# A linear-attention and token-mixing kernel on one core: another hand-written order, the products of v off GpSimd

## The chip, the cores and the metric

The kernel runs on one core of a Trainium2 chip. The metric is device time in microseconds (us) of one execution. TensorE is called PE in the profile (its weight loads PEld), VectorE DVE, ScalarE ACT, GpSimd POOL, and SyncE SP; SP issues all loads and stores here.

## The reference

Eight batches of eight heads; a sequence of 576 tokens, 64 numbers a head. First a linear attention with cosine weights, then a layer that mixes tokens:

```python
theta = np.pi / 2.0 * pos / S
def phi(x, c, s):
    r = np.maximum(x, 0.0)
    return np.concatenate([r * c, r * s], axis=-1)
q_p = phi(q, cos_w, sin_w); k_p = phi(k, cos_w, sin_w)
kv = np.einsum('bhsf,bhsd->bhfd', k_p, v)
z = np.sum(k_p, axis=2)
num = np.einsum('bhsf,bhfd->bhsd', q_p, kv)
den = np.einsum('bhsf,bhf->bhs', q_p, z)[..., None] + 1e-06
...
wq = x @ w_q; wk = x @ w_k
W_tok = scale * np.einsum('bsd,btd->bst', wq, wk)
mixed = np.einsum('bst,btd->bsd', W_tok, x)
return (np.maximum(mixed, 0.0) @ w_out)
```

Here `x` is num / den with the heads side by side, 8 x 576 x 512.

## The kernel before, in words

The work is cut into 16 groups H of four heads (two groups a batch). The order of all work is written out by hand: `ORDER` is a list of words such as `VS9a` or `KV11:6` or `RK9@A`. The letters name a step, the number its group, `a` or `b` one half of it, the number behind the colon the bank of PSUM that it starts in, and the letter behind `@` the engine (A ScalarE, V VectorE, G GpSimd). The kernel issues the steps in that order, and each engine works through its own in order; the framework adds the waits that the data and the buffers ask for.

One group passes through these steps:

- `LQ`, `LK`, `LV`: two loads of 288 KB each, issued by SP into one of four raw buffers.
- `RQ`, `RK` (lines 198 and 200): relu of q and k with conversion to bf16, on any of three engines, whole or by halves.
- The weighted v. The weights are put on v in place of k: `vtab` holds sine and cosine. Either `CV` converts v to bf16 (lines 204, 206, 208) and `VS` multiplies it on VectorE (line 229), or `VG` multiplies the raw v on GpSimd (line 243). The result is in one of two buffers `v2`.
- `KV` (line 280, or 270 in wide tiles): TensorE sums k'v over the tokens; `KE` moves the result to SBUF.
- `QT` (line 296, or 290 in wide tiles): TensorE transposes q; `QM` (line 315, wide 311) multiplies it by its weights on VectorE.
- `N` (line 335): numerator and denominator of half a group, g = 2H + r; `EP` (346 on ScalarE, 348 on VectorE) adds eps to the denominator, `RC` (line 367) or, for both halves at once, `RJ` (line 370) takes the reciprocal, `X` (line 382) multiplies: 32 such products of x.
- `XT` or `XR` (lines 395, 408) transposes x, `XE` copies it to SBUF.

A batch b then has `WK`, `KW`, `WQ`, `QW` (the two projections and their copies), `KX`, `XK`, `XA`, `XB` (the product of wk and x, and its copies across the halves of the partitions), four times `MX` and `ME` (mixing and its relu, line 478 and 489 or 491). Two batches make nine output tiles: `WO` (line 498, four products each), `OE` (the copy from PSUM) and `ST` (the store). `WU` (line 534) multiplies a constant tile of ones; nothing uses the result. `TK`, `TV`, `TQ`, `TW`, `T2`, `TZ`, `TI`, `TB` prepare tables and constants.

A step on one engine thus waits for its data and for its buffer to be free: `VS` and `VG` of group H wait until `KV` of group H - 2 has read its `v2`.

Of the kernel before, what the change touches and what calls it, by code (L numbers as in the profile page):

```python
# [29 lines left out]
RK2b@A WK0:4 VG5a RJ3 X6 RK2a@A QT2:0 KW0@A X7 LQ5a LQ5b LK5b LK5a LV4b LQ4b LV7b LV4a KV2:6 QM2  # L30
XT3:2 VG5b KE2@A RQ5@A XE3@V N4:0 N5:6 EP4@V RC4 WQ0:2 EP5@A X4 RK5b@A KX0:3 VG4b RK5a@A RC5 QT5:0
X5 XK0@A KV5:4 QW0@A QM5 XA0@A LK4b LQ4a LQ7a LK4a LQ7b LV7a XT2:2 XB0@A KE5@A CV7b@A MX1:6 VG4a
XE2@V N11:0 RQ4b@A N10:4 EP11@V ME1@A WK1:2 EP10@V RJ5 RQ4a@A X10 MX0:6 WQ1:3 KW1@A X11 RK4b@A
RQ7a@G QT4:4 KX1:2 ME0@A RK4a@G QM4 QW1@A RQ7b@G LK7b LK7a LQ6a LW3 LV6a LW2 KV4:6 XK1@A XA1@A VS7b
QT7:2 KE4@A MX3:4 VG7a N9:6 QM7 ME3@A N8:0 XB1@A WU13:4 EP9@A RK7@A MX4:4 EP8@V RJ4 XT5:2 X9 ME4@A
X8 KV7:6 CW3@A VG6a XE5@V MX6:4 KE7@A LW4 LQ6b LW5 LV6b LK6b LV9b LK6a XR4:0 ME6@A MX2:6 XE4@V N15:2
CW2@A N14:4 ME2@V RQ6a@A WK2:0 EP14@A EP15@V RQ6b@A MX5:6 CW4@G RJ7 WQ2:1 KW2@V ME5@A CW5@G X15
KX2:0 QW2@A VG6b X14 MX7:6 XK2@A QT6:2 ME7@A WO0:1 QM6 XB2@A RK6b@A LQ9b LQ9a LV9a LK8b LV8b LV8a
WO3:0 RK6a@A LK8a LK9b OE0:0@V XA2@G VG9b MX10:2 OE3:1@A MX8:6 KV6:4 ME8@V ME10@A XR7:0 KE6@V RQ9b@A
MX9:6 MX11:2 XE7@V WO8:4 ME9@A RQ9a@V ME11@A CV9a@G N12:6 LK9a LQ8a LQ8b LQ11a OE8:2@A N13:0 VS9a  # L40
QT9:2 LV11a WO2:4 VG8b QM9 CV8a@A WO10:5 EP12@A EP13@A LQ11b LK10a OE2:3@A RJ6 WO1:2 X13 OE10:4@A
RK8@G X12 WO6:3 RK9@A VS8a XR6:6 KV9:0 LV11b LQ10a LQ10b OE1:5@V RQ8b@G KV8:4 LV10a OE6:6@V KE9@A
RQ8a@G N18:0 XE6@V KE8@A LK11a N19:2 VG11a QT8:4 EP19@V EP18@V WK3:6 RJ9 RQ11b@A QM8 WO12:7 KW3@A
WO7:6 X19 LK11b LV10b LK10b OE12:7@A VG11b RK10a@A KX3:7 LV13b LV13a OE7:8@V RQ11a@A WQ3:2 X18 XK3@A
N17:4 XB3@A QW3@V N16:6 EP17@A VG10a LV12b ST1 XR9:0 RQ10@A EP16@V RJ8 WO9:2 XE9@V RK11@A WO11:3 X16
X17 QT11:0 VG10b LV12a LK13a LK12a OE11:9@A WO4:6 LK13b OE9:10@A QM11 XR8:2 LK12b OE4:11@A QT10:0
MX15:4 RK10b@A XE8@V KV11:6 CV13@G ME15@A QM10 ST6 WK4:2 XA3@A KE11@A CV12b@G KV10:4 KW4@A VS13
MX14:2 KE10@A MX13:0 N23:6 ME14@A KX4:4 ME13@A VS12b MX12:2 XK4@A WQ4:5 VG12a EP23@V ME12@A RC23 X23
N21:0 QW4@A N20:2 RK13@A EP21@V WO15:5 EP20@V RJ10 X20 LQ12b LQ13a LQ13b LQ12a ST3 ST11 WO16:4 ST12
OE15:5@A RK12b@G X21 XA4@A RK12a@G N22:2 XB4@A MX16:6 LV14b LQ14a OE16:6@A XR10:0 EP22@V RC22  # L50
RQ13a@G ME16@A X22 KV12:4 RQ13b@G KV13:6 XE10@V KE12@A RQ12b@A MX17:4 RQ12a@G LV15b LQ14b ST10
QT13:2 KE13@V ME17@A XR11:0 QM13 QT12:6 XE11@A WO13:4 QM12 WO14:5 LV15a LQ15a ST9 OE13:7@A CV14b@G
MX19:0 N26:2 LQ15b OE14:9@V N27:6 WK5:4 EP26@V EP27@V RJ13 VG15b X26 WO5:5 KW5@A ME19@A X27 ST0
LK15b LK15a KX5:4 OE5:1@A WQ5:0 XK5@V VS14b MX18:6 QW5@A XR13:4 ME18@A N24:2 VG15a N25:0 XE13@A
WO19:6 EP25@V RC25 X25 WO21:7 EP24@A XA5@A RC24 LV14a ST14 LK14a LK14b OE19:0@A X24 WO20:0 RQ14@G
OE21:10@A RQ15a@V XR12:6 ST21 OE20:4@A RQ15b@G MX20:2 QT14:4 XE12@V ME20@A RK15@G ST15 WO17:0 QM14
WK6:1 VG14a ST4 ST8 ST2 OE17:9@A QT15:6 KW6@A KV15:4 QM15 RK14a@A WQ6:1 XB5@A KE15@A KX6:0 QW6@A
RK14b@G MX22:6 XK6@A N31:4 ME22@V MX23:2 EP31@A ST16 ST17 ST7 ST5 KV14:0 ME23@A RC31 X31 MX21:6
KE14@A N30:2 ME21@A N28:0 EP30@V N29:4 RC30 EP28@A X30 WO22:6 EP29@A RJ14 WO23:7 X29 OE22:6@A XB6@A
X28 WO24:6 XA6@A OE23:8@A XR15:0 MX25:4 XR14:2 XE15@V ME25@A WO18:7 XE14@V WO26:0 ST23 ST22 OE24:1@V  # L60
WK7:1 OE18:9@V OE26:3@A MX26:2 KW7@V MX27:4 MX24:6 ME27@A WQ7:0 ME26@V KX7:1 ME24@A QW7@A WO25:2
XK7@A XB7@A XA7@G WO29:3 ST18 ST19 ST26 OE25:9@V MX28:0 MX29:6 MX30:4 ME28@V WO30:2 ME30@A ME29@V
ST25 ST24 ST20 OE29:3@A MX31:4 WO27:0 OE30:0@V ME31@A WO32:1 ST30 OE27:9@A WO34:0 ST29 ST27 OE32:1@V
# [6 lines left out]
def kernel(  # L70
# [256 lines left out]
    def N(g, ps, eng):  # L327
        H, r = divmod(g, 2)
        place["N", g] = ps
        nv = num4(ps)[:, r::2] if H in NUM_JOINT else num(ps)  # L330
        for u in range(SC):
            for s in range(2):
                for pr in range(2):
                    a = slice(H2 * pr, H2 * pr + H2)
                    nc.tensor.matmul(  # L335
                        nv[:, pr, u, :], qm_b[H % NQM][a, s, r, 2 * u:2 * u + 2, :],
                        kv_b[H % 2][a, r, pr if H in KV_WIDE else 0, s, 0:D + 1],
                        start=(u == 0 and s == 0), stop=(u == SC - 1 and s == 1))
# [4 lines left out]
    def EP(g, ps, eng):
# [3 lines left out]
        else:  # L347
            V.tensor_scalar(rec(g), den, EPS, None, op0=ALU.add)

    def EJ(H, ps, eng):  # L350
# [4 lines left out]
        else:  # L355
            V.tensor_scalar(dst, den, EPS, None, op0=ALU.add)

# [6 lines left out]
            op=ALU.mult)  # L364

    def RC(g, ps, eng):
        V.reciprocal(rec(g), rec(g))

    def RJ(H, ps, eng):
        V.reciprocal(rec_b[H % 4], rec_b[H % 4])  # L370
# [91 lines left out]

# [122 lines left out]
```

## Time and profile before

| | |
|---|---|
| runs | 124.07, 126.06, 126.73 us; median 126.06 |
| the profiled execution | 122.76 us, its span 120.9 us |
| busy in the span | PE 95.1, PEld 64.4, DVE 95.4, ACT 81.0, POOL 68.3 us |
| moved by DMA | 39.40 MB, mean 326 GB/s; 29.62 MB read, 9.44 MB written |
| granted clock of TensorE | 0.984 |

The span runs from the first to the last instruction of that one execution; the 1.9 us between it and the time of 122.76 lie around it. The busy shares are means over a start (loads come in), a middle and an end (output tiles). So the prediction reads them stage by stage.

### The profile page before, as it was taken

How to read it: one execution, taken by the hardware profiler on the slowest of the kernel's cores; microseconds unless marked ns; L12 is line 12 of the kernel's file. 1: busy time of each engine (PE TensorE's matmuls, PEld its weight loads, DVE VectorE, ACT ScalarE, POOL GpSimd, SP SyncE). 2: the span in 40 equal slices, each digit the busy share in tenths (PEclk: the TensorE clock that was granted, in tenths of full speed). 3: DMA queues.
4: the chain of work that ended last, by engine and by line, in shares of the span. 5: the costliest groups of instructions: out<-in, count | busy, mean ns of one | idle time of the engine just before them, and what ended most of it. 6: DMA issues, size and time to landing. Idle time of an engine off the chain costs nothing.

```text
span 120.9 us, 5257 instructions
## 1 busy us (share of the span) xinstructions
PE 95.1 (79%) x2243; PEld 64.4 (53%) x2256; DVE 95.4 (79%) x143; ACT 81.0 (67%) x157; POOL 68.3 (57%) x65
## 2 busy tenths in 40 slices
PE   0005779799794999959996999678999999999950
PEld 0004568587573686543954586254765875554410
DVE  0089887999799989999896999987979887946440
ACT  6307925769992989967479589766488886367210
POOL 7500079399997796995699919959994000010000
PEclk9999999999998599999999999999999999999999
DMA  3999999999999999999999999997352990466992
GB/s 99 371 389 404 396 361 355 394 390 390 395 392 378 370 367 386 397 391 389 387 393 399 398 396 338 378 400 280 110 180 89 342 350 14 174 266 260 373 386 111
DMA packets 20663, 39.40 MB, mean 326 GB/s; under 512 B 3232, under 2 KB 3232, under 8 KB 20640
## 3 DMA queue, kind: packets, MB, share of 16 engines
q1 hardware_dynamic: 20640, 39.07, 87.4%
q8 instruction: 17, 0.28, 0.9%
q14 instruction: 6, 0.05, 0.1%
HBM read 29.62 MB, written 9.44 MB: 323 GB/s over the span
## 4 chain that ended last, share of the span: by engine, by line
PE 44%; DMA 37%; issue 8%; DVE 5%; ACT 2%; SPq 1%; ACTq 0%; DVEq 0%
DMA vraw<-in_v_dram 27%; PE ps L498 23%; DMA kraw<-in_k_dram 10%; PE ps L335 4%; PE ps L280 4%; PE ps L408 3%; PE ps L478 2%; PE ps L428 2%; PE ps L455 2%; PE ps L441 2%; PE ps L296 2%; DVE x L382 1%; SPq L143 1%; DVE qm L311 1%; ACT rk L198 1%
## 5 line engine op out<-in xcount | busy, mean ns | idle before, releaser
L243 POOL TENSOR_TENSOR v<-vraw,vtab 128x1152 bf16<-128x1152 f32 x18 | 43.4, 2424 | 8.3 <-PE ps L280 3.9
L498 PE MATMUL ps<-wow,mix 128*128 128x512 bf16 x131 | 33.1, 380 | 2.2 <-issue 1.6
L382 DVE TENSOR_TENSOR x<-ps,rec 128x640 bf16<-128x640 f32 x32 | 25.3, 819 | 0.9
L498 PEld LDWEIGHTS <-mix 128*128 128x128 bf16 x144 | 12.8, 98 | 16.1 <-issue 2.6
L204 ACT COPY o<-ps 128x512 f32<-128x512 f32 x23 | 13.3, 587 | 11.1 <-PE ps L498 10.9
L315 DVE TENSOR_TENSOR qm<-ps,qtab 128x2304 bf16<-128x2304 bf16 x14 | 18.8, 1346 | 1.6 <-PE ps L296 1.4
L489 ACT ACTIVATE mix<-ps 128x576 bf16<-128x576 f32 x26 | 16.6, 652 | 3.3 <-PE ps L478 3.2
L335 PE MATMUL ps<-kvs,qm 64*128 64x65 bf16 x640 | 14.7, 199 | 1.6 <-DVE x L382 0.8
L200 POOL TENSOR_SCALAR rq<-qraw 128x576 bf16<-128x576 f32 (+1 forms) x13 | 9.0, 711 | 12.3 <-DVE x L382 9.8
L296 PE MATMUL ps<-ident,rq 64*128 64x64 bf16 x252 | 6.9, 199 | 11.6 <-ACT rq L198 10.2
L335 PEld LDWEIGHTS <-qm 64*128 64x128 bf16 x640 | 13.4, 100 | 4.0 <-issue 2.3
L198 ACT ACTIVATE rk<-kraw 128x576 bf16<-128x576 f32 (+1 forms) x16 | 13.5, 865 | 2.9 <-DMA kraw<-in_k_dram 2.8
L229 DVE TENSOR_TENSOR v<-vb,vtab 128x1152 bf16<-128x1152 bf16 (+1 forms) x11 | 15.0, 1381 | 0.4 <-ACT vb L204 0.4
L198 ACT ACTIVATE rq<-qraw 128x576 bf16<-128x576 f32 (+1 forms) x12 | 9.6, 802 | 5.5 <-DMA qraw<-in_q_dram 5.5
L280 PE MATMUL ps<-v,rk 64*64 64x130 bf16 x504 | 11.2, 232 | 2.0 <-issue 1.7
L208 DVE COPY xT<-ps 128x1280 bf16<-128x1280 bf16 (+1 forms) x13 | 10.4, 805 | 2.5 <-PE ps L408 1.9
L296 PEld LDWEIGHTS <-rq 64*128 64x128 bf16 x252 | 5.5, 100 | 12.6 <-ACT rq L198 10.4
L208 DVE COPY o<-ps 128x512 f32<-128x512 f32 x13 | 8.8, 686 | 4.3 <-PE ps L498 4.1
L280 PEld LDWEIGHTS <-rk 64*64 64x64 bf16 x504 | 8.7, 114 | 3.9 <-issue 2.3
L204 ACT CAST kvs<-ps 128x260 bf16<-128x260 f32 (+1 forms) x14 | 5.7, 408 | 7.4 <-PE ps L280 4.7
L206 POOL TENSOR_SCALAR kx<-kx 64x256 bf16<-64x256 bf16 x2 | 0.8, 401 | 16.8 <-ACT kx L204 16.8
L478 PE MATMUL ps<-wq,kx 64*128 64x288 bf16 x64 | 8.9, 297 | 0.0
(60 smaller groups left out, 127.0 us busy)
## 6 DMA issues: line engine op xcount, KB each, us to landing
vraw<-in_v_dram SPq DMA_DIRECT2D x32, 288.0 KB, 5.9
qraw<-in_q_dram SPq DMA_DIRECT2D x32, 288.0 KB, 5.9
kraw<-in_k_dram SPq DMA_DIRECT2D x32, 288.0 KB, 6.0
out_dram<-o SPq DMA_DIRECT2D x36, 256.0 KB, 3.4
...
```

The source lines that it names most:

```text
L198: A.activation(dst, s, AF.Relu)
L204: A.copy(dst, s)
L208: V.tensor_copy(dst, s)
L229: V.tensor_mul(v2_b[H % NV2][:, part, :, :, 0:D], vb_b[H % NPREP][:, part].unsqueeze(3).to_broadcast([P, n, C, 2, D]), vtab.unsqueeze(1).t ...
L243: G.tensor_mul(dst[:, part, :, :, 0:D], s[:, part].unsqueeze(3).to_broadcast([P, n, C, 2, D]), vtab.unsqueeze(1).to_broadcast([P, n, C, 2, ...
L280: nc.tensor.matmul(kv_v[o, r, :], rk_of(H)[a, pr, c, :], v2_b[H % NV2][a, pr, c, :, 0:D + 1], start=(c == 0), stop=(c == C - 1))
L296: nc.tensor.transpose(qt_v[:, r, c * H2:(c + 1) * H2], rq_b[H % NPREP][a, c, :, :], ident[a, a])
L315: V.tensor_mul(qm_b[H % NQM][:, :, :, 0:C, :].rearrange("p s r c d -> p s r (c d)"), qt_view(place["QT", H]).unsqueeze(1).to_broadcast([P, ...
L335: nc.tensor.matmul(nv[:, pr, u, :], qm_b[H % NQM][a, s, r, 2 * u:2 * u + 2, :], kv_b[H % 2][a, r, pr if H in KV_WIDE else 0, s, 0:D + 1], ...
L382: V.tensor_tensor(x_b[b % NX][:, :, 4 * h:4 * h + 4, :].rearrange("p u (w r) d -> p r w u d", r=2)[:, r], nv[:, :, :, 0:D], rec(g).to_broa ...
L489: A.activation(dst, s, AF.Relu, scale=scale_moe)
L498: nc.tensor.matmul(o, mix_b[bp % 2][:, m, rt * P:(rt + 1) * P], wow[:, m, :], start=(m == 0), stop=(m == NDM - 1))
```

## The change

`ORDER` is another list: nearly all steps stand in another place, many on another engine. No step is a `VG` any more; v is always converted by `CV` and multiplied by `VS`. By counts, of before and now: products of v on GpSimd 18 halves and none, on VectorE 3 whole and 8 halves, and 12 whole and 8 halves; relus and conversions of q, k and v on GpSimd 4 whole and 22 halves, and 12 whole and 36 halves; copies of xT on VectorE and ScalarE 13 and 3, and 4 and 12; copies of the output on VectorE and ScalarE 13 and 23, and 8 and 28; joint reciprocals 12 and 6, single ones 8 and 20. The groups with wide k'v tiles go from two to four, those with wide q transposes from two to seven. The two `WU` (four products of the constant tile in all) give way to one `WU174` at the head: 43 products of 128 x 128 by 384.

For five of the 32 half groups TensorE adds eps itself: two more products a group put a constant on the denominator in PSUM, and the reciprocal reads it there.

```diff
+EPS_HI = 134 * 2.0 ** -27
+EPS_LO = EPS - EPS_HI
 ORDER = """
-TZ TK TQ TV TI T2 LV1b LQ1a LV0a CV0a@G LV1a CV1@V RQ1a@V TB VS1 LK1a LV3b LK1b RK1@V LQ1b RQ1b@A
+LV0a TK TB WU174:0 LQ0a TQ LQ1b LV0b TZ TW LV1a LV1b TI LQ0b T2 LK0a TV LK0b LQ1a CV0a@A LK1a VS0a
...
+    EPS_PE = (0, 1, 3, 9, 13)
-    QT_WIDE = (3, 11)
-    KV_WIDE = (2, 3)
+    QT_WIDE = (0, 1, 3, 4, 8, 9, 15)
+    KV_WIDE = (1, 4, 5, 6)
...
+    ones_b = pool.tile([P, P], BF16, name="ones")
+    epsr_b = pool.tile([P, SC, 1], BF16, name="epsr")
...
-                        start=(u == 0 and s == 0), stop=(u == SC - 1 and s == 1))
+                        start=(u == 0 and s == 0),
+                        stop=(u == SC - 1 and s == 1 and g not in EPS_PE))
+        if g in EPS_PE:
+            for pr in range(2):
+                a = slice(H2 * pr, H2 * pr + H2)
+                nc.tensor.matmul(nv[:, pr, :, D:D + 1], ones_b[a], epsr_b[a],
+                                 start=False, stop=True)
...
     def RC(g, ps, eng):
-        V.reciprocal(rec(g), rec(g))
+        V.reciprocal(rec(g), num(place["N", g])[:, :, :, D:D + 1] if g in EPS_PE else rec(g))
...
     def TB(i, ps, eng):
         V.memset(wc, 1.0)
+        V.memset(ones_b, 1.0)
+        for r, e in enumerate((EPS_HI, EPS_LO) * 2):
+            V.memset(epsr_b[32 * r:32 * r + 32], e / 32)
```

The order on GpSimd, around groups 9 and 8, before (`vb` is the converted v, `v2` the weighted v, here with buffer numbers: raw buffers 1 and 0 belong to groups 9 and 8, 3 to group 11):

```order
L206 TENSOR_SCALAR kx0_99<-kx0_99 64x256
L243 TENSOR_TENSOR v21_82<-vraw1_72,vtab_118 128x18x64
L206 TENSOR_SCALAR vb1_80<-vraw1_72 128x576
L243 TENSOR_TENSOR v20_81<-vraw0_71,vtab_118 128x18x64
L200 TENSOR_SCALAR rk0_75<-kraw0_63 128x1152
L200 TENSOR_SCALAR rq0_77<-qraw0_67 128x9x64 x2
L243 TENSOR_TENSOR v21_82<-vraw3_74,vtab_118 128x18x64 x2
```

And now, around the same groups:

```order
L206 TENSOR_SCALAR rq1_78<-qraw1_68 128x2x9x64
L206 TENSOR_SCALAR rk0_75<-kraw2_65 128x9x64
L212 TENSOR_SCALAR vb1_80<-vraw1_72 128x576
L206 TENSOR_SCALAR rk1_76<-kraw1_64 128x1152
L212 TENSOR_SCALAR vb0_79<-vraw0_71 128x1152
L206 TENSOR_SCALAR rq0_77<-qraw0_67 128x9x64 x2
```

The products of v have left this engine; relus and conversions of both groups stand there one behind the other.

The order on VectorE for the same two groups, before (`qm` is the weighted q, `rec` the reciprocals, `o` output tiles):

```order
L208 COPY xT1_94<-ps_115 128x2x2x5x64
L200 TENSOR_SCALAR rq1_78<-qraw1_68 128x9x64
L229 TENSOR_TENSOR v21_82<-vb1_80,vtab_118 128x18x64
L315 TENSOR_TENSOR qm1_84<-ps_115,qtab_119 128x4x576
L370 RECIPROCAL rec2_89<-rec2_89 128x20
L382 TENSOR_TENSOR x1_92<-ps_115,rec2_89 128x2x5x64 x2
L229 TENSOR_TENSOR v20_81<-vb0_79,vtab_118 128x18x64
L208 COPY o5_108<-ps_115 128x512
L208 COPY o6_109<-ps_115 128x512
```

And now:

```order
L317 TENSOR_TENSOR qm1_84<-ps_115,qtab_119 128x2x576 x2
L235 TENSOR_TENSOR v21_82<-vb1_80,vtab_118 128x36x64
L360 TENSOR_SCALAR rec2_89<-ps_115 128x10
L379 RECIPROCAL rec2_89<-ps_115 128x10
L379 RECIPROCAL rec2_89<-rec2_89 128x10
L394 TENSOR_TENSOR x1_92<-ps_115,rec2_89 128x2x5x64 x2
L235 TENSOR_TENSOR v20_81<-vb0_79,vtab_118 128x36x64
L214 COPY xT1_94<-ps_115 128x2x2x5x64
```

Both products of v are whole now, twice the elements, and the copies of output tiles that stood behind them have gone to ScalarE.

More of the change, by code (lines that the diff above doesn't have):

```diff
@@ L30 @@
[L30 to L63, printed above, removed]
@@ new lines @@
+RQ13b@G LV10a N16:0 WO12:4 CV11@G EP16@A OE5:2@A LV13a RC17 X17 WO10:2 OE12:5@A RK11a@G RC16 RQ10@A
+X16 WO11:3 RQ13a@G LK15a LV15a VS11a OE10:6@A MX15:0 MX14:4 ST12 QT10:6 VS11b ME14@A LV12a WO3:2
+ME15@A QM10 RK10b@G LK12a KV11:4 RK10a@G LK13b XR8:0 OE3:7@V KE11@A MX13:6 XE8@A N23:4 CV10@V WO7:2
+EP23@V ME13@V OE11:8@A WK4:0 OE7:9@A RC23 ST11 X23 WO9:3 KW4@A ST5 VS10 LK14b MX12:4 OE9:10@A N22:0
+LQ12b QT13:6 ME12@A ST8 KX4:3 EP22@V QM13 RQ12a@A LK13a WQ4:2 LV15b CV13a@A KV10:4 CV12a@A RC22
+LV14b WO1:6 KE10@V RK12@G CV13b@A LV14a X22 XK4@A WO16:7 XA4@A VS13 CV12b@A LQ15b N21:0 XB4@A N20:4
@@ new lines @@
+OE1:2@A LK14a EP21@V WO17:3 CV15a@G EP20@V RJ10 ST3 X21 RK13b@G WO14:6 OE17:8@A ST1 X20 RQ12b@G
+QW4@A XR11:0 LK15b OE14:1@A RK13a@G OE16:5@V MX17:2 XR10:4 WO15:6 CV15b@G XE11@V XE10@A VS12 KV13:0
+OE15:11@A WK5:7 ME17@A ST15 VS15 KV12:4 LQ15a KW5@A KE13@A ST6 QT12:6 KE12@A MX16:0 CV14a@G LQ14b
+MX18:2 QM12 ME16@A KX5:4 LQ14a CV14b@G ME18@A WQ5:5 XK5@A VS14 MX19:0 N26:6 N27:2 EP26@A ME19@A
+WO13:4 RK15@G EP27@V QW5@A RJ13 X27 WO21:0 OE13:11@A RQ15b@G X26 XB5@A N24:4 RK14@A RQ15a@G N25:2
+EP24@V XR13:6 RC24 XA5@G X24 WO20:1 EP25@A OE21:0@A RC25 XE13@A X25 RQ14@G QT15:4 WO19:0 QM15
@@ L66 @@
+ME27@V WO26:5 XK7@A XB7@G WO29:4 XA7@G OE26:4@A MX29:6 MX28:0 OE29:10@V MX30:2 WO22:5 ME30@A ME29@V
+ST29 ME28@A ST18 MX31:2 WO27:4 OE22:6@A ME31@V ST22 WO30:5 OE27:8@V ST7 ST26 WO32:2 OE30:10@V WO34:4
+ST30 OE32:1@A ST27 WO35:5 OE34:6@A ST32 WO28:4 ST34 OE35:4@V WO33:2 ST35 OE28:10@V WO31:5 ST28
+OE33:8@A ST33 OE31:6@A ST31
 """
```

30 lines of the change are left out of this document (24 added, 6 removed).

## The prediction

> **What bounds the kernel now.** I read the page first, then the busy time by stretches, cut at three products of x (the 4th, 24th and 32nd of the 32 instructions of L382, which end at 22.2, 80.1 and 101.9 us).
>
> ```profile
> span 120.9 us, 5257 instructions
> PE 95.1 (79%) x2243; PEld 64.4 (53%) x2256; DVE 95.4 (79%) x143; ACT 81.0 (67%) x157; POOL 68.3 (57%) x65
> GB/s 99 371 389 404 396 361 355 394 390 390 395 392 378 370 367 386 397 391 389 387 393 399 398 396 338 378 400 280 110 180 89 342 350 14 174 266 260 373 386 111
> core 0: us, PE busy (x) PEld busy (x) DVE busy (x) ACT busy (x) POOL busy (x), PEclk, DMA share, GB/s
> 0.00:22.20 22.20, 9.83 (x235) 7.98 (x235) 13.70 (x20) 10.86 (x20) 9.08 (x23) 1.00 0.96 342
> 22.20:80.10 57.90, 50.24 (x1359) 35.47 (x1369) 54.00 (x82) 46.13 (x91) 47.75 (x34) 0.97 1.04 386
> 80.10:101.90 21.80, 20.48 (x525) 13.71 (x518) 18.30 (x30) 16.57 (x34) 11.10 (x7) 1.00 0.59 216
> 101.90:116.60 14.70, 14.58 (x141) 7.27 (x142) 9.38 (x14) 6.87 (x13) 0.40 (x1) 1.00 0.70 268
> 79.27 0.83 DVE L382 TENSOR_TENSOR x<-ps,rec 128x640 bf16<-128x640 f32 x1
> 100.34 1.56 DVE L382 TENSOR_TENSOR x<-ps,rec 128x640 bf16<-128x640 f32 x2
> ```
>
> The reader should see a relay. From 22.2 to 80.1 us VectorE works 54.0 of 57.9 us while the loads run at 386 GB/s: both are nearly full, and ScalarE and GpSimd have room. From 80.1 to 101.9 TensorE is full (20.48 of 21.8) with VectorE close behind (18.3). From 101.9 on TensorE alone sets the end: 14.58 of 14.7 us, 13 output tiles and the last group's mixing. In both orders exactly 13 WO steps, one WK, WQ and KX and eight MX stand behind the last product of x, so I leave that tail and the 19.0 us behind 101.9 as they are. The question is when the last product of x is done, and for that VectorE's work ahead of it: 13.70 + 54.00 + 18.30 = 86.0 us busy, 15.9 idle, 7.4 of it behind 22.2.
>
> **Work that moves on and off VectorE ahead of the last product of x.**
>
> ```profile
> L243 POOL TENSOR_TENSOR v<-vraw,vtab 128x1152 bf16<-128x1152 f32 x18 | 43.4, 2424 | 8.3 <-PE ps L280 3.9 <-issue 2.5 <-DMA vraw<-in_v_dram 1.9
> L229 DVE TENSOR_TENSOR v<-vb,vtab 128x1152 bf16<-128x1152 bf16 x8 | 11.1, 1399 | 0.4 <-ACT vb L204 0.4
> L229 DVE TENSOR_TENSOR v<-vb,vtab 128x2304 bf16<-128x2304 bf16 x3 | 4.0, 1331 | 0.0
> L208 DVE COPY xT<-ps 128x1280 bf16<-128x1280 bf16 (+1 forms) x13 | 10.4, 805 | 2.5 <-PE ps L408 1.9 <-PE ps L395 0.6
> L208 DVE COPY o<-ps 128x512 f32<-128x512 f32 x13 | 8.8, 686 | 4.3 <-PE ps L498 4.1
> L370 DVE RECIPROCAL rec<-rec 128x20 f32<-128x20 f32 x12 | 3.3, 276 | 1.2 <-ACT rec L346 0.8
> L367 DVE RECIPROCAL rec<-rec 128x10 f32<-128x10 f32 x8 | 1.7, 212 | 0.2
> L208 DVE CAST vb<-vraw 128x1152 bf16<-128x1152 f32 x1 | 0.8, 760 | 6.6 <-DMA vraw<-in_v_dram 6.6
> L311 DVE TENSOR_TENSOR qm<-ps,qtab 128x1152 bf16<-128x1152 bf16 x4 | 2.8, 752 | 0.5 <-PE ps L290 0.4
> L315 DVE TENSOR_TENSOR qm<-ps,qtab 128x2304 bf16<-128x2304 bf16 x14 | 18.8, 1346 | 1.6 <-PE ps L296 1.4 <-ACT qtab L177 0.2
> 88.27 0.75 DVE L229 TENSOR_TENSOR v<-vb,vtab 128x1152 bf16<-128x1152 bf16 x1
> ```
>
> The 18 products of v on GpSimd (43.4 us) go. VectorE makes all: 12 whole ones at 1.33 us and 8 halves at 0.75 (an undisturbed half, last row), 22.0 us, where the 11 of before took 11.1 + 4.0 = 15.1: **+6.9**. Copies of xT ahead of the last product of x fall from 11 to 3: 8 x 0.805 = **-6.4**. Copies of o there fall from 5 to 2: 3 x 0.686 = **-2.1**. Reciprocals: 20 singles and 6 doubles, 20 x 0.212 + 6 x 0.276 = 5.9, against 8 x 0.212 + 12 x 0.276 = 5.0: **+0.9**. Three half conversions of v come; no row shows one here, but a whole one takes 0.76, so each lies between 0.38 and 0.76, nearer to the half since elements decide: **+1.4**. Five more q products of the wide kind cost 2 x 0.752 - 1.346 = 0.16 each, +0.8; the remaining copies and relus that come and go cancel this. Sum: **+0.7**. Counted by work, VectorE is exactly as loaded as before. The eps of five groups by TensorE saves five small adds ahead of the reciprocals, spread on two engines, and costs TensorE two five-column products a group; I set it at nothing.
>
> **The lock.** What the durations hide is in three products of before:
>
> ```profile
> 36.29 2.36 POOL L243 TENSOR_TENSOR v<-vraw,vtab 128x1152 bf16<-128x1152 f32 x1 [0.18 <-DMA vraw<-in_v_dram]
> 36.45 2.82 DVE L229 TENSOR_TENSOR v<-vb,vtab 128x1152 bf16<-128x1152 bf16 x1
> 52.04 1.68 DVE L229 TENSOR_TENSOR v<-vb,vtab 128x1152 bf16<-128x1152 bf16 x1
> 72.74 2.93 DVE L229 TENSOR_TENSOR v<-vb,vtab 128x1152 bf16<-128x1152 bf16 x1
> 53.19 1.54 POOL L200 TENSOR_SCALAR rk<-kraw 128x1152 bf16<-128x1152 f32 x1
> 87.24 1.15 POOL L200 TENSOR_SCALAR rk<-kraw 128x1152 bf16<-128x1152 f32 x1
> L200 POOL TENSOR_SCALAR rq<-qraw 128x576 bf16<-128x576 f32 x12 | 7.9, 674 | 12.2 <-DVE x L382 9.8 <-PE ps L335 2.3
> ```
>
> A half product that meets a GpSimd product takes 2.82, 1.68 or 2.93 us instead of 0.75: it stands until the other ends. The 5.2 us of waiting are in the 15.1 above. It works the other way too: the relu that began under VectorE's product at 53.19 took 1.54 where an undisturbed one takes 1.15. In the new order GpSimd makes 12 whole and 36 half conversions, 12 x 1.15 + 36 x 0.67 = 38 us, mean 0.79, about as much of the time as its products filled before. So I carry the rate over: 3 of 11 products hit gives 5.5 of 20, and each loses the same share of the other's length, (2.07 + 0.93 + 2.18) / 3 / 2.38 = 0.73, so 0.73 x 0.79 = 0.57 us. **+3.1.** Bounds: 0 if conversions do not block, and 20 x 0.79 = 16 if each product meets one.
>
> The trace is not of one mind: the product at 88.27 began 0.12 us before the relu of 87.24 ended and still took 0.75. Taken by itself this row makes the term 0 and the sum +0.1. The Trainium skill ("SBUF — State Buffer", section "Who interferes with whom") says that a VectorE instruction with two inputs in SBUF and a GpSimd instruction that reads SBUF exclude one another, whatever the operation, and the first to start wins; by that rule the 3.1 stands and the sum is the one below. The three long products agree with it; no row of before shows a product held by a conversion.
>
> **Waits that change queue.** GpSimd's products stood 3.9 us until kv products freed their buffer and 1.9 for loads of v (L243's row), with nobody behind them who mattered. VectorE's own stood 0.4. Now every product waits in VectorE's queue, with the q products and x products behind it, and TensorE's kv and num steps behind those. Bounds: 0.4 x 9/11 = +0.3, and +5.8 if all of GpSimd's waiting moves. I take **+1.0**, near the VectorE row, because a busy engine arrives late at its waits.
>
> **TensorE.** From the 24th product of x on, 20 output tiles remain instead of 22; a tile's four products take about 0.87 us:
>
> ```profile
> 110.37 6.22 PE L498 MATMUL ps<-wow,mix 128*128 128x512 bf16 x28
> 67.43 0.67 PE L290 MATMUL ps<-ident,rq 128*128 128x128 bf16 x9
> 69.60 0.44 PE L296 MATMUL ps<-ident,rq 64*128 64x64 bf16 x18 [0.25 <-DVE qm L311]
> 25.59 1.19 PE L270 MATMUL ps<-v,rk 64*128 64x260 bf16 x18 [0.18 <-DVE x L382]
> 29.89 0.72 PE L280 MATMUL ps<-v,rk 64*64 64x130 bf16 x36
> 10.25 0.66 PE L296 MATMUL ps<-ident,rq 64*128 64x64 bf16 x18 [10.25 <-ACT rq L198]
> L534 PE MATMUL ps<-warm 64*128 64x384 bf16 x4 | 1.5, 468 | 0.0
> L204 ACT COPY xT<-ps 128x1280 bf16<-128x1280 bf16 x3 | 3.7, 1230 | 0.9 <-PE ps L408 0.9
> ```
>
> 28 products in 6.22 us is 0.22 each. Two tiles fewer is -1.7, and one more xT transpose and one more mixing step give back some 0.5: **-1.2**, since this stretch is TensorE's. The wide transposes cost 0.23 us each (0.67 against 0.44), the wide kv products 0.47 (1.19 against 0.72); ahead of 80 us both lie under VectorE, and TensorE has 7.7 us to spare there. Without that cover the five wide transposes and the two wide kv steps more would cost 2.1.
>
> At the front 43 products of the warm tile now run ahead of everything on TensorE. The first 18 transposes took 0.66 us at 10.25 and 0.44 later, so the front's transposes, kv and num gain when the engine is already fast: a few tenths on the path, **-0.4**. The block itself costs nothing if it is over when the first relu of q is there (about 10 us). By the output tile's rate 43 x 384 columns take 43 x 0.22 x 0.75 = 7.1 us; by the four warm products' row 43 x 0.468 = 20. I take the first, as the 0.468 spans an overlapped start. The Trainium skill ("TensorE: Matmul & The Clock Gate", "What's actually happening") says that the engine starts at half its clock and rises after some 3.4 us of work; an estimate by that page is 10 products in 3.4 us and 33 in 5.4, an end near 10 us. Both leave the sum as it is, the row with 20 does not, and is a rival.
>
> On SP's queue the last load stands behind the 24th product of x's place instead of the 27th, with nine stores ahead in both; the loads are not later. ScalarE gets nine more xT copies (9 x 1.23 = 11) and loses sixteen relu steps of 0.7 to 1.2; it has 11.8 us to spare between 22.2 and 80.1, and that is the cover.
>
> **Sum**: +0.7 + 3.1 + 1.0 - 1.2 - 0.4 = **+3.2 us**. The profiled execution took 122.76 (span 120.9 and 1.9 around it), so its like would be 126.0. The runs' median is 126.06, 3.3 above that execution; the forecast for the median is **129.3**.
>
> **Rivals.** *The order gains*: the lock does not hold against conversions (the row at 88.27) and v's buffers come early (so neither 3.1 nor 1.0), and with GpSimd free for relus q and k come sooner, so that half of VectorE's 7.4 idle us goes: 3.2 - 3.1 - 1.0 - 3.7 = -4.6, **121.5**. It decides at 22 us: VectorE must stay within 54 us up to the 24th product of x. For it speaks that GpSimd was busy 47.75 of 57.9 us there; against it that the loads were at 386 GB/s.
> *Nothing nets out*: VectorE's lock waits fall into its 7.4 idle us, **126**.
> *The conversions of v come late*: 13 conversion steps of v are in GpSimd's line, each behind up to two relus (1.15 + 0.67); if half of them hold a product some 0.85 us longer, 5.5 more, **134.8**. Against it: VectorE waited 0.4 so far.
> *The warm block stays slow*: at 0.468 it ends at 21 us, and half of the 11 us lost is not regained, 126.06 + 3.2 + 5.5 = **134.8** too. The row of 0.468 speaks for it, the output tiles' rate against it.
>
> **How the numbers follow.** Forecast 0.35, gain 0.30, nothing 0.18, late conversions 0.12, slow warm block 0.05. A change of 2% (2.5 us) is about what a measurement of this kernel can tell from none. Slower by more: 0.33 + 0.12 + 0.05 = 0.50; within: 0.18 + 0.02 = 0.20; faster: 0.30. The forecast's own range is 127.5 to 131.5; 121 to 135 takes in the rivals' centres and leaves out the rest.
>
> **What would show it.** Right: products of v on VectorE with some five to seven well above 1.33 and 0.75, their sum near 25 us; VectorE busy over 56 us between the 4th and 24th product of x; the last product of x near 105 us and a tail of 19. Wrong: products all at 1.33 and 0.75, the last product of x ahead of 101, or a first transpose behind 12 us.

## The result, and the profile after

The changed kernel takes 127.14 us (median of four runs, 126.14 to 129.11) against 125.53 for the kernel before (four runs, 124.07 to 126.73): slower, by a ratio of 1.0324, 95% interval 1.0257 to 1.0391. The ratios here leave out each kernel's disturbed, longer executions, so they are not the ratios of the medians; the profiles of the third, ninth and tenth experiments come from such executions and are used for what an engine has to do, not for their ends. The profiled execution took 126.67 us, 3.9 more than the one of before.

The page of the changed kernel, its span, busy times and the chain that ended last:

```profile
span 124.9 us, 5208 instructions
PE 106.2 (85%) x2224; PEld 69.9 (56%) x2224; DVE 96.4 (77%) x156; ACT 84.3 (68%) x154; POOL 51.3 (41%) x72
PE 55%; DVE 27%; issue 8%; ACT 7%; DVEq 0%; ACTq 0%
```

The same chain of the kernel before:

```profile
PE 44%; DMA 37%; issue 8%; DVE 5%; ACT 2%; SPq 1%; ACTq 0%; DVEq 0%
```

GpSimd's 68 us became 51, while VectorE's 95 and ScalarE's 81 did not fall. The loads have left the chain and VectorE has come in: before, work kept up with the loads; now it does not.

The changed kernel's busy times by stretches, cut at the same three products of x (4th, 24th and 32nd):

```profile
core 0: us, PE busy (x) PEld busy (x) DVE busy (x) ACT busy (x) POOL busy (x), PEclk, DMA share, GB/s
0.00:22.20 22.20, 16.42 (x266) 10.58 (x266) 13.24 (x28) 11.59 (x21) 7.43 (x22) 1.00 0.96 337
22.20:84.20 62.00, 54.37 (x1286) 38.30 (x1285) 56.01 (x90) 47.38 (x88) 33.52 (x38) 0.94 0.99 356
84.20:106.00 21.80, 20.20 (x560) 14.00 (x553) 19.02 (x31) 16.99 (x32) 9.53 (x12) 1.00 0.69 244
106.00:120.70 14.70, 14.70 (x126) 7.04 (x124) 8.15 (x13) 7.53 (x14) 0.80 (x2) 1.00 0.65 248
```

Put beside the four rows of before, this says where the time went. The front (22.2 us), the last stretch of x (21.8) and the tail (18.9 behind 106.0, 19.0 before) are equal. All of the loss lies in the second row: 62.0 us for what took 57.9. There VectorE works 56.0 instead of 54.0 us and idles 6.0 instead of 3.9, and the loads run at 356 GB/s instead of 386. Up to the last product of x, VectorE is busy 13.24 + 56.01 + 19.02 = 88.3 us (before 86.0) and idle 17.7 (before 15.9): +2.3 and +1.8, together the 4.1 us.

Groups of the changed kernel, with shapes kept apart:

```profile
L235 DVE TENSOR_TENSOR v<-vb,vtab 128x2304 bf16<-128x2304 bf16 x12 | 17.5, 1465 | 0.0
L206 POOL TENSOR_SCALAR rq<-qraw 128x576 bf16<-128x576 f32 x16 | 13.8, 872 | 9.6 <-DMA qraw<-in_q_dram 5.7 <-ACT rq L204 3.7
L549 PE MATMUL ps<-warm 128*128 128x384 bf16 x43 | 9.9, 408 | 1.5 <-DVE warm L540 1.5
L235 DVE TENSOR_TENSOR v<-vb,vtab 128x1152 bf16<-128x1152 bf16 x8 | 6.5, 842 | 6.3 <-ACT vb L210 4.8 <-POOL vb L212 1.5
L214 DVE CAST vb<-vraw 128x576 bf16<-128x576 f32 x3 | 1.7, 587 | 0.0
```

The 20 products of v take 17.5 + 6.5 = 24.0 us where undisturbed ones would take 22.0. Which ones are held shows in the changed kernel's timeline, GpSimd and VectorE side by side (start, duration):

```profile
53.87 1.15 POOL L212 TENSOR_SCALAR vb<-vraw 128x1152 bf16<-128x1152 f32 x1
54.29 1.94 DVE L235 TENSOR_TENSOR v<-vb,vtab 128x2304 bf16<-128x2304 bf16 x1
57.96 1.35 DVE L235 TENSOR_TENSOR v<-vb,vtab 128x2304 bf16<-128x2304 bf16 x1
70.03 2.12 DVE L235 TENSOR_TENSOR v<-vb,vtab 128x1152 bf16<-128x1152 bf16 x2
89.70 1.15 POOL L206 TENSOR_SCALAR rk<-kraw 128x1152 bf16<-128x1152 f32 x1 [0.45 <-DMA kraw<-in_k_dram]
89.91 2.15 DVE L235 TENSOR_TENSOR v<-vb,vtab 128x2304 bf16<-128x2304 bf16 x1
```

A conversion runs to 53.87 + 1.15 = 55.02; the product that began under it ends at 56.23, 1.21 us later. The other runs to 90.85, its product to 92.06: again 1.21 later. A free product takes 1.35. So the product stands until the conversion is over, but for 0.14 us; whether these lie at its start or in how the two ends are recorded is not shown.

### The profile page after: what moved, and what is told of

Read it like the earlier page. It is cut to its first block, busy times and chain, and to the rows that moved or that the text cites. A ratio compares the mean times of both kernels' runs of the same rounds, so it can differ in the third digit from the quotient of the medians.

```text
span 124.9 us, 5208 instructions
## 1 busy us (share of the span) xinstructions
PE 106.2 (85%) x2224; PEld 69.9 (56%) x2224; DVE 96.4 (77%) x156; ACT 84.3 (68%) x154; POOL 51.3 (41%) x72
## 4 chain that ended last, share of the span: by engine, by line
PE 55%; DVE 27%; issue 8%; ACT 7%; DVEq 0%; ACTq 0%
PE ps L510 19%; PE ps L549 8%; DVE x L394 8%; DVE qm L317 6%; PE ps L341 6%; DVE v L235 4%; PE ps L440 4%; PE ps L286 4%; PE ps L453 3%; PE ps L467 3%; DVE qm L321 3%; PE ps L490 3%; ACT mix L501 2%; PE ps L420 2%; DVE rec L379 1%
## 5 line engine op out<-in xcount | busy, mean ns | idle before, releaser
L235 DVE TENSOR_TENSOR v<-vb,vtab 128x2304 bf16<-128x2304 bf16 (+1 forms) x20 | 24.0, 1216 | 6.3 <-ACT vb L210 4.8
L206 POOL TENSOR_SCALAR rq<-qraw 128x576 bf16<-128x576 f32 (+1 forms) x19 | 17.3, 915 | 12.3 <-DMA qraw<-in_q_dram 8.4
L206 POOL TENSOR_SCALAR rk<-kraw 128x576 bf16<-128x576 f32 (+1 forms) x16 | 15.4, 970 | 14.9 <-DMA kraw<-in_k_dram 7.5
L510 PEld LDWEIGHTS <-mix 128*128 128x128 bf16 x144 | 12.6, 97 | 14.8 <-issue 1.6
L212 POOL TENSOR_SCALAR vb<-vraw 128x576 bf16<-128x576 f32 (+1 forms) x13 | 12.7, 980 | 11.1 <-DMA vraw<-in_v_dram 7.9
L501 ACT ACTIVATE mix<-ps 128x576 bf16<-128x576 f32 x25 | 15.9, 651 | 1.6 <-PE ps L490 1.5
L210 ACT COPY xT<-ps 128x1280 bf16<-128x1280 bf16 (+1 forms) x12 | 14.4, 1202 | 0.7 <-PE ps L420 0.5
L321 DVE TENSOR_TENSOR qm<-ps,qtab 128x2304 bf16<-128x2304 bf16 x9 | 12.1, 1351 | 0.6 <-ACT kvs L210 0.5
L317 DVE TENSOR_TENSOR qm<-ps,qtab 128x1152 bf16<-128x1152 bf16 x14 | 9.9, 748 | 2.3 <-PE ps L296 2.3
L549 PE MATMUL ps<-warm 128*128 128x384 bf16 x43 | 9.9, 408 | 1.5 <-DVE warm L540 1.5
L214 DVE COPY o<-ps 128x512 f32<-128x512 f32 x8 | 5.5, 687 | 4.2 <-PE ps L510 2.3
L549 PEld LDWEIGHTS <-warm 128*128 128x128 bf16 x43 | 5.0, 119 | 5.9 <-issue 2.9
```

Of the source, the lines that this page charges most:

```text
L206: eng.tensor_scalar(dst, s, FMAX, 0.0, op0=ALU.min, op1=ALU.max)
L210: A.copy(dst, s)
L212: G.tensor_scalar(dst, s, 1.0, 1.0, op0=ALU.mult, op1=ALU.mult)
L235: V.tensor_mul(v2_b[H % NV2][:, part, :, :, 0:D], vb_b[H % NPREP][:, part].unsqueeze(3).to_broadcast([P, n, C, 2, D]), vtab.unsqueeze(1).t ...
L317: V.tensor_mul(qm_b[H % NQM][:, :, r, 0:C, :], q_t[:, r].unsqueeze(1).to_broadcast([P, 2, C, H2]), qtab)
L321: V.tensor_mul(qm_b[H % NQM][:, :, :, 0:C, :].rearrange("p s r c d -> p s r (c d)"), qt_view(place["QT", H]).unsqueeze(1).to_broadcast([P, ...
```

## The experiments

Twelve kernels were run. Each ratio is against the kernel before, run on the same chip; the changed kernel itself was not run again beside them.

**1. Is it the clock?** In the changed kernel's profile TensorE's granted clock is 0.50 from about 25 to 31 us. 29 more products of the constant tile (the expectation counts 26) fill TensorE's gaps ahead of it, between 11.6 and 24.6 us.

```diff
-QT0:0 ... KV0:2 ... N0:0 ... KV1:4 ... XR1:4 ... QT2:2
+QT0:0 WU14:4 ... KV0:2 WU22:4 ... N0:0 WU18:6 ... KV1:4 WU34:6 ... XR1:4 WU10:6 ... QT2:2 WU30:6
```

> The changed kernel with 26 more products of the constant tile on TensorE, in its gaps between 12 and 25 us, so that its clock is not halved at 25 to 31 us. Nothing else differs. Theory A (VectorE's work and its waits for GpSimd made the change slower; the halved clock is hidden): ratio to the kernel before 1.03, the 24th product of x still ends near 84 us. Theory B (the halved clock delays the chain, 3 us): granted clock 1.00 at 25 to 31 us, the 24th product of x near 81.5 us, span near 122, ratio 1.01.

Measured: 123.83, 126.32, 127.02 and 128.23 us. The profiled execution is the shortest, and the only one that counts for a ratio: 1.009 of the kernel before, without an interval. From its page:

```profile
PEclk9999999999999999999999999999999999999999
```

The dip is gone, and in this execution most of the loss too: the 24th product of x ends at 82.3 us instead of 84.2, and the span is 122.1 instead of 124.9, about as the second theory expected. Against that theory stands an execution of the changed kernel itself, at a granted clock of 1.000 without the extra products: it took 126.14, only 0.5 less than the profiled one with the dip. How much of the loss the dip makes is left open by these runs.

**2. The hole in the loads.** SP's queue stands still from 46.5 to 51.2 us, because a load waits for a relu on GpSimd, which stands behind a copy of kx (`XA2`) that waited 3.5 us for ScalarE. The copy goes to ScalarE.

```diff
-N14:4 XA2@G
+N14:4 XA2@A
```

> The changed kernel with one 0.4 us copy of kx (batch 2) moved from GpSimd to ScalarE: on GpSimd it stood 3.5 us waiting ahead of the relu of group 9, and SP issued no load from 46.5 to 51.2 us because the next load waits for that relu. Theory A and B (no load is on the chain then): the hole in the loads is smaller, the span stays within 0.5 us of 124.9, ratio 1.03. Theory C (late loads through GpSimd's queue are the loss): span 2 to 3 us less, ratio 1.01.

The moved bytes by slices of the span, of the changed kernel:

```profile
GB/s 115 357 371 388 404 375 340 391 390 391 391 388 389 387 383 388 134 302 393 400 392 388 238 342 351 337 349 344 306 203 0 184 346 311 239 115 142 405 379 168
```

and of the experiment:

```profile
GB/s 112 341 388 403 396 378 333 387 389 389 395 385 384 387 392 390 390 231 348 371 247 301 380 333 383 250 321 243 389 390 73 171 336 342 280 85 177 402 363 171
```

The slice of 134 GB/s is filled; others open later. The four executions took 124.16 to 127.16 us; the ratio, made as the others are, is 1.014, from two executions and without an interval. The span of the profiled one is 122.8 us, 2.1 less than the changed kernel's, which is what the third theory expected and not the first two. But little of it lies where the hole was: the 24th product of x ends at 83.8 instead of 84.2 us, and the 25th at 91.7 instead of 93.4. Between these two the product of v that was held in the changed kernel (2.15 us at 89.91) is free:

```profile
89.02 1.35 DVE L235 TENSOR_TENSOR v<-vb,vtab 128x2304 bf16<-128x2304 bf16 x1
```

So half of the loss is gone here, and the profile puts more of it down to this one meeting than to late loads. Why the two no longer meet is not shown.

**3. The block at the head, alone.** The 43 products go to the head of the kernel before.

```diff
+TB WU174:6 TZ TK TQ TV ...
-RQ1a@V TB
+RQ1a@V
```

> The kernel before with the block of 43 products of the constant tile at its head, the one part of the change alone. My prediction gave it -0.4 us: ratio 0.997. If a fast start were worth more (TensorE ran at half speed from 10 to 22 us), the 4th product of x would end 1.5 us earlier than 22.2 and the ratio be 0.985; if the block holds up the first transposes, it would be 1.005 or more.

```profile
1.45 9.86 PE L534 MATMUL ps<-warm 128*128 128x384 bf16 x43 [1.45 <-DVE warm L528]
11.24 0.44 PE L296 MATMUL ps<-ident,rq 64*128 64x64 bf16 x18
```

Ratio 1.0126 (1.005 to 1.0202): the wrong sign. The block lasts until 11.31 us, and the first transposes, ready at 10.25 in the kernel before, run at 11.24. They are faster then (0.44 instead of 0.66), and in this profile the 4th product of x ends at 22.40 us instead of 22.22: most of the lost microsecond is made up by then, but the gain that a fast start was to bring is not there. Where the 1.3% arises behind that is not shown.

**4. The lock by itself.** A kernel that computes nothing of the reference and stores zeros: products of v (L204), conversions on GpSimd (L175), q products of 2304 elements (L290), whole conversions on VectorE (L183) and GpSimd products (L218) in stretches, alone and against one another. In short, with the number of repeats:

```diff
+VS0a x6 VS0 x4                                  (products alone)
+RK0a@G x4 RK0@G x3                              (conversions alone)
+VS0a x8 VS0 x6     against RK0a@G x10 RK0@G x7
+QM0 x4 CV0@V x4    against RK0a@G x8 RK0@G x8
+VS0a x6            against VG1a x5
```

> Not the computation: the output is zeros, and only one group's loads, conversions and products are made, repeated in five stretches: products of v on VectorE alone; conversions on GpSimd alone; both at once; q products (one input in PSUM) and whole conversions on VectorE against conversions on GpSimd; products of v on VectorE against products on GpSimd. If conversions block products as GpSimd's products do (my term of 3.1 us): alone 0.75 and 1.33 us for a product, 0.67 and 1.15 for a conversion, and together both kinds grow, sums adding up to the wall time. If they do not (the row at 88.27 us): both keep their durations side by side. The q products keep 1.35 in both theories.

Its timeline, a row for each stretch (start, duration, engine, count at the end):

```profile
10.62 10.24 DVE L204 TENSOR_TENSOR v<-vb,vtab 128x1152 bf16<-128x1152 bf16 x10
22.07 6.61 POOL L175 TENSOR_SCALAR rk<-kraw 128x576 bf16<-128x576 f32 x7
29.51 25.28 POOL L175 TENSOR_SCALAR rk<-kraw 128x576 bf16<-128x576 f32 x17
29.84 21.48 DVE L204 TENSOR_TENSOR v<-vb,vtab 128x1152 bf16<-128x1152 bf16 x14
56.32 5.53 DVE L290 TENSOR_TENSOR qm<-ps,qtab 128x2304 bf16<-128x2304 bf16 x4
57.24 17.30 POOL L175 TENSOR_SCALAR rk<-kraw 128x576 bf16<-128x576 f32 x16
61.77 5.62 DVE L183 CAST vb<-vraw 128x1152 bf16<-128x1152 f32 x4
76.05 13.23 DVE L204 TENSOR_TENSOR v<-vb,vtab 128x1152 bf16<-128x1152 bf16 x6
77.30 14.19 POOL L218 TENSOR_TENSOR v<-vraw,vtab 128x1152 bf16<-128x1152 f32 x5
```

Alone, 6 halves and 4 wholes take 10.24 us, and 7 conversions 6.61. Together, 14 products that would take 8 x 0.75 + 6 x 1.33 = 14.0 take 21.48, and 17 conversions worth 10 x 0.67 + 7 x 1.15 = 14.8 take 25.28. The two engines' work, 28.8 us, needs 25.3: they nearly take turns. So conversions hold products and products hold conversions. Products of q, which read PSUM, are not held: 5.53 / 4 = 1.38. The row at 88.27 that seemed to speak against this in the kernel before agrees now: its product met only the last 0.12 us of a conversion, less than the 0.14 found above.

**5. Only the products of v move.** In the kernel before, all 18 `VG` become a conversion on GpSimd and a `VS` a few words later.

```diff
-QT3:0 VG3a ... WK0:4 VG5a ... (18 in all)
+QT3:0 CV3a@G ... EP1@V VS3a ... WK0:4 CV5a@G ... LQ5a VS5a ...
```

> The kernel before with its own order, only each of the 18 products of v on GpSimd replaced by a conversion on GpSimd at the same place and a product on VectorE up to eight words later. Theory A (VectorE and its waits bound the stretch from 22 to 80 us): VectorE gains 18 x 0.75 = 13.5 us of work and loses 5.2 of waiting; 7.4 us were idle, so the last product of x comes 4 to 8 us later, ratio 1.03 to 1.06. Theory B (VectorE is not the bound, TensorE's clock and order are): ratio within 1.00 to 1.02.

Ratio 1.0379 (1.0245 to 1.0513). Its busy times between the products of x:

```profile
22.30:83.40 61.10, 49.86 (x1377) 34.94 (x1381) 59.43 (x96) 46.57 (x92) 27.49 (x36) 1.00 1.05 385
83.40:106.70 23.30, 20.73 (x514) 13.55 (x503) 20.05 (x34) 16.55 (x34) 4.76 (x5) 1.00 0.43 156
```

VectorE works 59.43 of 61.10 us (before 54.0 of 57.9): here it is the bound. GpSimd gained 28 us (68 to 40 busy) that nobody waited for.

**6. Twelve halves back on GpSimd.** In the changed kernel, v of groups 4, 6, 8, 11, 14 and 15 is multiplied by GpSimd at the place of its conversion; at some of these places the product stands ahead of the kv products of an earlier group, so these use other values of v.

```diff
-XE3@A CV4@G ... LQ6a VS4 ...
+XE3@A VG4b VG4a ... LQ6a ...
```

> The changed kernel with the products of v of groups 4, 6, 8, 11, 14 and 15 (12 halves) given back to GpSimd, in the place of their conversions; the rest of the order stands. VectorE loses about 9.6 us, GpSimd gains 21. Theory A: VectorE's stretch shrinks and the kernel gets faster, ratio 0.99 to 1.01. Theory B: no gain, ratio 1.03. If GpSimd's queue becomes the bound (relus of q and k behind 2.4 us products), slower, 1.04 or more.

```profile
PE 105.6 (81%) x2224; PEld 68.7 (53%) x2224; DVE 88.2 (68%) x149; ACT 84.3 (65%) x154; POOL 68.8 (53%) x76
```

Ratio 1.0778 (1.059 to 1.0966). VectorE is relieved by 8 us (96.4 to 88.2), and the kernel is much slower. What TensorE waits for there (total us, times, longest):

```profile
PE ps L246 <- POOL rk L166: 3.3, 3, 1.3
PE ps L246 <- POOL v L209: 2.1, 1, 2.1
PE ps L236 <- POOL rk L166: 2.1, 2, 1.3
```

The kv products wait for GpSimd's relus and products: its line is full of conversions that others need, and a product of 2.4 us stands in front of them. So at these places the new order has no room for them on GpSimd.

**7. Narrow tiles.** `QT_WIDE` and `KV_WIDE` of the changed kernel are emptied.

```diff
-    QT_WIDE = (0, 1, 3, 4, 8, 9, 15)
-    KV_WIDE = (1, 4, 5, 6)
+    QT_WIDE = ()
+    KV_WIDE = ()
```

> The changed kernel with no wide tiles: q transposes and kv products all narrow, the order as it stands. TensorE saves 7 x 0.23 + 4 x 0.47 = 3.5 us, VectorE 7 x 0.16 = 1.1, ScalarE some 0.9 in copies of kv. If these lie on the path, the span falls by 1 to 2 us, ratio 1.02; if they are covered, as I predicted, 1.03.

Ratio 1.0351 (1.0256 to 1.0447), the changed kernel's own within its interval: no gain or cost of the wide tiles can be told.

**8. eps on VectorE.** `EPS_PE` is emptied, and five `EP` steps on VectorE are put back.

```diff
-    EPS_PE = (0, 1, 3, 9, 13)
+    EPS_PE = ()
-N0:0 ... EP2@A ... RC2 ... XE5@A ... EP12@V
+N0:0 EP0@V ... EP2@A EP1@V ... RC2 EP3@V ... XE5@A EP9@V ... EP12@V EP13@V
```

> The changed kernel with eps added on VectorE for all groups (five more adds of 0.16 us), none by TensorE. Predicted as nothing: ratio 1.03 (span within 0.8 us of 124.9). If the short way by TensorE is worth more, 1.04.

Ratio 1.0194 (1.0074 to 1.0313), which overlaps the 1.0257 to 1.0391 of the changed kernel: no gain from eps by TensorE is seen, and whether it costs is open. Here too the product of v at 89.05 us is free (1.35 us), and the span is 122.6.

**9. Only the copies move.** In the kernel before, nine copies of xT and three of the output go from VectorE to ScalarE.

```diff
-XE0@V ... XE3@V ... XE2@V ... XE5@V ... XE4@V ... OE0:0@V ... OE6:6@V
+XE0@A ... XE3@A ... XE2@A ... XE5@A ... XE4@A ... OE0:0@A ... OE6:6@A
```

> The kernel before with nine copies of xT (groups 0, 2 to 5, 7 to 10) and three output copies (tiles 0, 1, 6) moved from VectorE to ScalarE, at their places; the products of v stay. VectorE loses 9 x 0.81 + 3 x 0.69 = 9.3 us, ScalarE gains 12.8. This is the other half of the trade in the change. Theory A (VectorE bounds the middle): faster, ratio 0.97 to 0.99. Theory D (the copies are on a chain of waits, and a copy of 1.23 us on ScalarE in place of 0.81 gives back what VectorE saves): ratio 0.995 to 1.01.

Measured 1.0376 (1.0245 to 1.0506): not a gain but a loss, although VectorE has 9 us less to do (86.1 busy). Busy times from 36 to 50 us, of the kernel before:

```profile
36.00:50.00 14.00, 12.18 (x314) 8.52 (x303) 13.14 (x18) 11.22 (x24) 11.05 (x8) 0.88 1.03 378
```

and of this one:

```profile
36.00:50.00 14.00, 10.49 (x330) 7.80 (x322) 8.70 (x16) 13.89 (x27) 9.30 (x7) 1.00 1.04 380
```

ScalarE went from 11.22 to 13.89 of 14 us, full, and VectorE from 13.14 to 8.70, waiting. VectorE was not the only bound of the kernel before: ScalarE had only 2.8 us free here.

**10. Both moves in the old order.**

```diff
-VG3a ... XE0@V ...
+CV3a@G ... VS3a ... XE0@A ...
```

> The kernel before with both halves of the trade: 18 products of v from GpSimd to VectorE (as in the run without GpSimd products) and nine xT copies and three output copies from VectorE to ScalarE. VectorE's work is then that of the changed kernel, in the order of before and without the warm block, the wide tiles and eps by TensorE. Theory A: about half of the 1.038 comes back, ratio 1.00 to 1.02. Theory D: ratio 1.03 to 1.045. Were the new order itself the loss in the changed kernel, 1.00.

Ratio 1.0461 (1.0344 to 1.0579). VectorE is busy as before (95.7 us), ScalarE has 92.1 and GpSimd 40.3. The two moves do not cancel. The lock is not the price: what its 29 products of v take beyond 0.75 and 1.35 us comes to 2.0 us, where the three held ones of before lost 5.2. ScalarE's room is gone, as in the ninth experiment.

**11. Three repairs of the changed kernel.** A block of 35 products, the kx copy on ScalarE, eps on VectorE (with the five `EP` steps of the eighth experiment).

```diff
-TB WU174:0 ... N14:4 XA2@G
+TB WU142:0 ... N14:4 XA2@A
-    EPS_PE = (0, 1, 3, 9, 13)
+    EPS_PE = ()
```

> The changed kernel with three repairs: 35 products in the first block in place of 43 (it ends near 9.5 us, before the first relu of q is there), the kx copy of batch 2 on ScalarE (no hole in the loads at 47 to 51 us), and eps on VectorE for all groups. If each is worth what its single run showed (about 0.5, 1 and 1.3 per cent), ratio 1.00 to 1.01; if those were chance, 1.025 to 1.035.

```profile
1.45 8.34 PE L549 MATMUL ps<-warm 128*128 128x384 bf16 x35 [1.45 <-DVE warm L540]
10.63 0.68 PE L296 MATMUL ps<-ident,rq 128*128 128x128 bf16 x9 [0.84 <-ACT rq L204]
```

Ratio 1.0179 (1.0019 to 1.0339). The block ends in time, and the first transposes run 0.6 us sooner. Together the three may be worth a per cent; the kernel before stays the fastest. The product of v behind the 24th product of x is free here as well.

**12. The whole rotation in the old order.** The tenth kernel, with sixteen relu steps more moved from ScalarE to GpSimd, as many as the change moves, though not all the same ones.

```diff
-RK5b@A ... RK5a@A ... RQ4a@A ... RK7@A ... RK9@A ... RQ11b@A ... RK13@A ... RQ12b@A
+RK5b@G ... RK5a@G ... RQ4a@G ... RK7@G ... RK9@G ... RQ11b@G ... RK13@G ... RQ12b@G
```

> The kernel before, in its own order, with all three moves of the change: the eighteen half products of v from GpSimd to VectorE, the nine copies of x's transposes and three output copies from VectorE to ScalarE, and sixteen conversions (relu) of k and q from ScalarE to GpSimd. Only the list of steps differs from e10; the order of the products on TensorE stays that of the kernel before. Theory A (the loss is the price of the rotation: VectorE's sum does not fall and its products of v wait on GpSimd's conversions, whatever the order): 1.02 to 1.04 of the kernel before, near the changed kernel's 1.032, with ScalarE back from 92 us to about 84 and GpSimd near 51. Theory B (the new order itself loses the time, the rotation is free once ScalarE is relieved): 1.00 to 1.01. Theory C (the conversions on GpSimd come late and hold up TensorE more than ScalarE's relief brings): it stays at e10's 1.046 or above.

Its busy row, and its busy times between the products of x:

```profile
PE 95.6 (76%) x2256; PEld 64.8 (51%) x2256; DVE 97.6 (77%) x149; ACT 82.4 (65%) x153; POOL 55.3 (44%) x81
```

```profile
22.50:84.20 61.70, 50.66 (x1380) 36.16 (x1383) 54.16 (x83) 47.11 (x88) 42.67 (x52) 0.97 1.02 374
84.20:107.60 23.40, 20.77 (x514) 13.61 (x502) 19.72 (x33) 16.70 (x34) 4.34 (x6) 1.00 0.47 171
```

Ratio 1.048 (1.0392 to 1.0568). ScalarE came back from 92.1 to 82.4 us and it brought nothing, as the third expectation had it; the first ends at 1.04, just inside the interval. The rotation costs without the new order, and at least as much: the second stretch takes 61.7 us here, 62.0 in the changed kernel, 57.9 before. So the new order is not needed for the loss; by the next stretch (23.4 here, 21.8 there) it may take part of it back. What it would do without the rotation no run shows.

## Why the prediction was right, point by point

The forecast was slower by 3.2 us in the profiled execution; it was 3.9. The time lies within 121 to 135; the forecast's own range began at 127.5, and 127.14 is just outside it. The place was the one given, VectorE's busy time between the 4th and 24th product of x with an unchanged tail (18.9 us); the lock came out smaller than its term, and the waits, TensorE and the front worse than theirs, so it is in part luck that the sum came this near. The terms fared as follows.

**Work on VectorE, +0.7, and the lock, +3.1: together +3.8, measured +2.3.** The lock is real (experiment 4), but the products lose less to it: 12 x (1.465 - 1.33) + 8 x (0.842 - 0.75) = 2.4 us by the group means, 2.0 by the groups' sum. Three places are held for 0.6 to 0.8 us each (the rows at 54.29, 70.03, 89.91), not 5.5 for 0.57. The step that failed is that GpSimd would be busy about as much of the time as before: from 22.2 to 84.2 us it works 33.5 of 62, while before it was 47.75 of 57.9. What remains, between -0.1 and +0.3, is the work by the forecast's count (+0.7); half conversions take 0.587 in the mean, within their bounds, and 0.45 undisturbed. That count hides something: its 15.1 us for the products of before contain 5.2 us of lock. Without what the lock took, VectorE's work up to the last product of x rose from 80.8 to 86.2 us, and the lock itself fell from 5.2 to 2.1 (2.2, 2.0 and 4.0 in the old order, experiments 5, 10 and 12). So in sum the lock is not what made the kernel slower than before.

The Trainium skill ("SBUF — State Buffer", "Who interferes with whom") calls the ports that VectorE and GpSimd share an exclusive lock, and says that whoever issues first gets them for the whole instruction while the other fully blocks. The trace agrees, but for the 0.14 us. By the same section a conversion on VectorE in a two-port mode can be held as well: in experiment 4 whole ones took 5.62 / 4 = 1.40 instead of 0.76.

**Waits that change queue, +1.0; measured about +2.1** in the second stretch (6.0 us idle for 3.9). The place was wrong: products of v wait there only 0.65 us for their data (before not at all), and their other 5.6 us of waiting lie ahead of the 4th product of x, where no time was lost. The added idle time is in VectorE's short steps, behind others' lateness; the longest:

```profile
65.44 0.42 DVE L214 CAST kx<-ps 128x256 bf16<-128x256 f32 x1 [1.74 <-PE ps L467]
```

**TensorE, -1.2.** Two output tiles fewer in the stretch from the 24th to the last product of x left it at 21.8 us, as before. But where the product of v at about 89 us is free, in the second, eighth and eleventh experiments, this stretch takes 20.2, 19.9 and 20.2 us; where it is held, in the first and the seventh (2.31 and 2.22 us), 20.9 and 21.9. From the 24th to the 25th product of x it is 7.9 us in the three free ones and 8.9 to 9.2 in the changed kernel and the two held ones. So the changed kernel's profile has about 1.2 us there that hang on this one meeting, and without them the -1.2 fits. That it was the two tiles is not shown. In the old order, moving the products of v alone makes the stretch 23.3 us and the whole rotation 23.4 (experiments 5 and 12).

**The loads, not later.** They were: of the 102 loads the 72nd is issued at 55.4 us instead of 52.2 and the last at 88.4 instead of 86.6. That this cost time is not shown: in the second experiment the last is issued at 88.4 too.

**The front, -0.4; measured 0, and +1.3% for the block alone.** The term that failed is the block's length, put at 7.1 us by the output tile's rate per column for all 43 products. It took 9.93. Rows of the changed kernel:

```profile
1.45 9.93 PE L549 MATMUL ps<-warm 128*128 128x384 bf16 x43 [1.45 <-DVE warm L540]
11.92 1.42 DVE L317 TENSOR_TENSOR qm<-ps,qtab 128x1152 bf16<-128x1152 bf16 x2 [2.25 <-PE ps L296]
82.67 1.56 DVE L394 TENSOR_TENSOR x<-ps,rec 128x640 bf16<-128x640 f32 x2
104.47 1.56 DVE L394 TENSOR_TENSOR x<-ps,rec 128x640 bf16<-128x640 f32 x2
```

and the block alone, cut at 7.15 us (the product that lies across the cut counts in both rows):

```profile
core 0: us, PE busy (x) PEld busy (x), PEclk, DMA share, GB/s
1.45:7.15 5.70, 5.70 (x18) 2.69 (x19) 1.00 0.94 320
7.15:11.38 4.23, 4.23 (x26) 2.35 (x24) 1.00 1.02 374
```

The first 18 products take 0.32 us each, the other 25 take 0.17, which is the forecast's rate (0.22 x 0.75). So the rate was right once TensorE was fast, and the 5.7 us before that were left out. The block ends at 11.38, and VectorE waits 2.25 us for the first transposes. By the 4th product of x both kernels stand at 22.2, so the late start was made up, and nothing was won. The two rows of x are the marks: 84.2 and 106.0 us, where the forecast said about 105. The Trainium skill ("TensorE: Matmul & The Clock Gate", "What's actually happening") led to an estimated end near 10 us, nearer than the 8.6 of the rate but still 1.4 short: its half clock fits the first 18 products, but they lasted 5.7 us here, not some 3.4.

**Wide tiles covered, eps at nothing:** no run speaks against the first (experiment 7); what eps is worth stays open (experiment 8).

**The median.** The forecast of 129.3 added the 3.3 us by which the median of before lay above its profiled execution. Of the changed kernel the median lies 0.5 above (127.14 and 126.67). That step, not the sum, made the forecast 2.2 us high and put the time outside its own range.

**What the forecast did not say.** It took ScalarE's 11.8 spare us as cover for nine xT copies. Spread over 57.9 us they are no reserve where the copies fall: experiment 9 fills ScalarE from 36 to 50 us (13.89 of 14). In the changed kernel sixteen relus have left ScalarE for GpSimd (ScalarE is busy 12.15 of the same 14 us there), and on GpSimd they meet the products of v. What stays open is why this last move brings nothing in the old order (experiments 10 and 12), where no engine is full in the second stretch: VectorE 54.2, TensorE 50.7, ScalarE 47.1, GpSimd 42.7 of 61.7 us. So that the rotation costs is shown, and by which waits it costs is in part open.
